# One denominator set per segment, gate rows behind the first logit slot, and numerators normalized on GpSimd in a gated mix of linear-memory attention and a GeGLU layer

## The chip, the cores and the metric

The kernel runs on one core of one Trainium2 chip. The metric is the device time of one execution in microseconds; the median of three runs of the kernel before is 274.99 us (274.38 to 275.15). PE is the matmul engine (TensorE), PEld its weight loads, DVE VectorE, ACT ScalarE, POOL GpSimd, and SP the engine that issues most of the transfers.

## The reference

`x` is 2048 x 512 in bfloat16. The output is `g * a + (1 - g) * b`, with a gate per row, an attention part `a` and a feed-forward part `b`:

```python
g = _sigmoid((x * gate_w).sum(-1, keepdims=True))
h = _gelu(x @ w_gate) * (x @ w_up)                 # 512 -> 1792
b = h @ w_down                                     # 1792 -> 512
# attention: 32 heads of 16, four segments of 512 rows, head gate sigmoid(beta)
for s in range(N):                                 # N = 4
    logits = jnp.einsum('bhqd,bhkd->bhqk', qs, ks) * scale + mask   # causal in the segment
    a_dot = jnp.einsum('bhqk,bhkd->bhqd', _softmax(logits, axis=-1), vs)
    pq = phi(qs)                                   # t + 1 where t > 0, else exp(t)
    num = jnp.einsum('bhld,bhde->bhle', pq, M)
    den = jnp.einsum('bhld,bhd->bhl', pq, z)[..., None] + 1e-06
    outs.append(gh * (num / den) + (1.0 - gh) * a_dot)
    M = M + jnp.einsum('bhld,bhle->bhde', phi(ks), vs)
    z = z + jnp.einsum('bhld->bhd', phi(ks))
a = concat(outs) @ wo
```

`M` (16 x 16 per head) and `z` (16 per head) carry the memory over the segments; segment 0 has no memory part.

## The kernel before

**A schedule made at build time.** The kernel adds tasks with `add(engine, cost, fn, prio, deps, alloc, frees)` and lets `Sched.plan` simulate the five engines with these costs; `emit` writes the tasks in the planned order. Each engine then runs its own instructions strictly in that order. What is written before the tasks (memsets, masks, first loads) stands ahead of all tasks in its engine's queue. `NUPS` says how many of the 56 up groups are filler work in each segment, `SEED` perturbs priorities, and `RINGS` gives the number of buffers of each ring tile. `ps` is the whole PSUM, eight banks that the planner hands out.

**Stage 1 (to about 66 us).** x of segment 0 is transposed on PE against an identity (L550); DVE and ACT copy the result into `xT` (L316, two copies each), and 16 matmuls (L565) compute the keys of segment 0. Then follow q, v, and the 28 pairs of gate projections with their GELU on ACT (L475, L647). Among them stand one small matmul for the head gates (L666: `hot8` spreads the eight rows of `beta8` onto 128 rows) and, ahead of the pairs of segment 3, the 16 matmuls of the row gates (L601: `gwB` is gate_w, repeated 32 times). DVE transposes the row gates (L610), POOL spreads them over the partitions with 32 small copies into `G2` and `omz` (L618, L619), and ACT applies the exponential at the start of stage 2 (L624, L625).

**Stage 2 (66 to 260 us).** 80 logit slots: four segments, four chunks of eight heads, five slots each. In a slot, four 32-row strips of the array compute logits of four heads (L735, mode "row"); ACT takes the exponential into `pT` (L757), and POOL zeroes what the causal mask excludes (L766). Between the slots PE does filler groups (L479) in which four matmuls, each for 32 output columns of the array, run side by side: up projections (`wup`), the down projection with `wo` behind it into the same bank, and q, k, v of the next segments. Every fifth slot opens two `pv` groups (L785), which need the masked `pT`; DVE transposes their result, divides by its sum, adds the memory part and transposes it into `xT`.

**The memory part.** `phi` makes pq and pk with an exponential on ACT and two DVE operations, `m_update` accumulates `M` and `z` in `Macc` and writes them, masked by block, into `Mbd` and `zbd`. `mem_den` is a dense product of the four chunks of pq with `zbd`, all accumulated into one bank: 4 chunks x 4 column strips = 16 matmuls. `mem_num` makes four matmuls per chunk with `Mbd`. The numerators are transposed on DVE into `Tm` (L977) and multiplied there with the reciprocal denominators `rm` (L981).

**Loads.** SP issues the weights in the order written, then gate_w, beta, `wup`, `wo` and, once the first transposes are done, `wdn`. `f_wo` scales `wo` by one minus the head gate on DVE (L681).

Of the kernel before, what the change touches and what calls it, by code (L numbers as in the profile page):

```python
# [10 lines left out]
ALU = mybir.AluOpType  # L11
# [26 lines left out]
NUPS = (28, 10, 9, 9)  # L38
ATT = 5
SEED = 1  # L40
# [248 lines left out]
def kernel(  # L289
# [22 lines left out]
    def copy(e, dst, src):  # L312
        if e == "ACT":
            nc.scalar.activation(dst, src, AF.Copy)
        else:
# [6 lines left out]
    RINGS = {"qT": 3, "kT": 3, "kO": 3, "pT": 12, "E": 1, "Q1": 1, "pq": 3,  # L322
             "pkT": 1, "pk": 2, "T": 2, "r": 2, "N": 2, "rm": 1, "Tm": 1, "Nm": 3,
             "osb": 3, "tt": 1}
# [34 lines left out]
    beta8 = ctile("beta8", [8, NCH])  # L359
    bd = ctile("bd", [P, 8, DH])  # L360
    hot8 = ctile("hot8", [8, 8, DH])
# [3 lines left out]
    zbd = ctile("zbd", [P, NCH * (P + 2)])  # L365
# [5 lines left out]
    omg = ctile("omg", [P, NCH], F32)  # L371
    ebr = ctile("ebr", [P, NCH], F32)
    tb = ctile("tb", [P, NCH], F32)
# [13 lines left out]
    gwB = p1.tile([P, FC, 32], BF, name="gwB", tag="gwB")  # L387
# [4 lines left out]
    nc.vector.memset(warm, 0.0)  # L392
    x0r = x2[0:L, :].rearrange("(kt p) d -> p kt d", p=P)
# [11 lines left out]
    nc.sync.dma_start(beta8[:, :], A_beta.rearrange("(c h) -> h c", h=8))  # L405
    load_w(nc.sync, wup, B_w_up)
    load_w(nc.sync, wo, A_wo)

    def ext(at):
# [17 lines left out]
    nc.vector.memset(zbd[:, :], 0.0)  # L427
# [8 lines left out]
                            compare_op=ALU.is_ge, fill=0.0, base=DH - 1, channel_multiplier=-1)  # L436
    nc.gpsimd.memset(vz[1][:, :, :], 1.0)
# [158 lines left out]
    def gate_rows(prio):  # L596

        def mms(t):
            for fc in range(FC):
                for s in range(NSEG):  # L600
                    nc.tensor.matmul(t[32 * s:32 * s + 32, :], lhsT=gwB[:, fc, :],  # L601
                                     rhs=xT[:, fc, s * L:(s + 1) * L], start=(fc == 0),
                                     stop=(fc == FC - 1), tile_position=(0, 32 * s),
                                     skip_group_check=True)
        g, box = group("gz", 4 * MM, mms, prio, a_x + [TAB["gwB"]], mode="col")
        tl = {}

        def f_tt(e, t):
            tl["tt"] = rtile("tt", [P, QB, 32], F32, p1)
            nc.vector.transpose(tl["tt"][:, :, :].rearrange("p a b -> p (a b)"), t[:, :])  # L610

        def f_sp(e):
            z = tl["tt"]
            for s in range(NSEG):
                src = slice(32 * s, 32 * s + 32)
                for j in range(4):
                    dst = slice(32 * j, 32 * j + 32)
                    nc.gpsimd.tensor_copy(G2[dst, s, :], z[src, :, 0])  # L618
                    nc.gpsimd.tensor_copy(  # L619
                        omz[dst, s, :],  # L620
                        z[src, :, :].rearrange("p (kt a) b -> p a kt b", a=4)[:, j, :, 0])

        def f_ex(e):
            nc.scalar.activation(G2[:, :, :], G2[:, :, :], AF.Exp)  # L624
            nc.scalar.activation(omz[:, :, :], omz[:, :, :], AF.Exp)  # L625

        def f_om(e):
            nc.vector.tensor_scalar_add(omz[:, :, :], omz[:, :, :], 1.0)
            nc.vector.reciprocal(omz[:, :, :], omz[:, :, :])
        for s in range(NSEG):  # L630
            read_x[s].append(g)
        tt = evac("DVE", g, box, f_tt, alloc=["tt"])
        TAB["zsp"] = add("POOL", 4000, f_sp, deps=[tt], prio=6, frees=[("tt", tt)])

        def later():
            TAB["g2"] = add("ACT", 500, f_ex, deps=[TAB["zsp"], TAB["first_x"]], prio=2)
            TAB["omz"] = add("DVE", 250, f_om, deps=[TAB["g2"]], prio=5)
        TAB["later"] = later
# [26 lines left out]
    def f_bps(t):  # L665
        nc.tensor.matmul(t[:, 0:NCH], lhsT=hot8[:, :, :].rearrange("p a b -> p (a b)"),  # L666
                         rhs=beta8[:, :], start=True, stop=True)
# [5 lines left out]
    def f_eb(e):  # L673
        nc.vector.reciprocal(ebr[:, :], omg[:, :])
        nc.vector.tensor_scalar_add(ebr[:, :], ebr[:, :], -1.0)
        for c in range(NCH):
            nc.vector.tensor_scalar_mul(bdeb[:, c, :, :], bd[:, :, :], ebr[:, c:c + 1])

    def f_wo(e):
        for c in range(NCH):  # L680
            nc.vector.tensor_scalar_mul(wo[:, c, :], wo[:, c, :], omg[:, c:c + 1])  # L681
# [6 lines left out]
    for s in range(NSEG):  # L688
        if s == 3:
            gate_rows(-960 + 20 * s)  # L690
        for hp in range(HS // 2):
            gate_pair(s, hp, -959 + 20 * s + hp)
            if s == 1 and hp == HS // 2 - 1:
                g, box = group("bps", 60, f_bps, -922, [a_be])
                t_tb = evac("ACT", g, box, lambda e, t: nc.scalar.activation(
                    tb[:, :], t[:, 0:NCH], AF.Tanh, scale=0.5), cost=250)
                t_om = add("DVE", 100, f_omg, deps=[t_tb], prio=5)
                t_eb = add("DVE", 1200, f_eb, deps=[t_om], prio=5)
                t_wo = add("DVE", 1300, f_wo, deps=[t_om, a_wo], prio=7)
# [4 lines left out]
    opened = add("EXT", 0, reopen, deps=list(GM.values()) + [TAB["zsp"]])  # L704
# [3 lines left out]

    def lhs_rhs(s, c, e, j, kt, qb, nq):
        pr, i = c // 2, c % 2  # L710
        a = slice(32 * j, 32 * j + (DH if e == 0 else 32))
        k = QK[("k" if e == 0 else "o", s, pr)]
        return (k[a, i, kt * P:(kt + 1) * P],
                QK[("q", s, pr)][a, i, qb * P:(qb + nq) * P])

    def logit_slot(s, t):
# [20 lines left out]
        deps = [EVQK[("q", s, c)]]  # L737
        if w <= 2:
            deps.append(EVQK[("k", s, c)])
        if w >= 2:  # L740
            deps.append(EVQK[("o", s, c)])
# [5 lines left out]
        if w == 4 and c % 2 == 1:  # L747
            pr = c // 2
            frees = [(n + "T" if n != "o" else "kO", first_ev[(n, s, pr)]) for n in "qko"]
            if s == 0:  # L750
                frees = [((r, pr) if r == "kT" else r, x) for r, x in frees]
# [22 lines left out]
    def pv_group(s, c, e):  # L774
# [4 lines left out]
        def mms(t):  # L779
            for w, kt, qb, nq, at in ((w0, 0, 0, 4, 0), (w0 + 1, 1, 1, 2, 0),  # L780
                                      (w0 + 1, 1, 3, 1, 3), (2, 2, 2, 2, 2 * e),
                                      (w0 + 1, 3, 3, 1, 2)):
                for j in range(4):
                    h = 8 * c + 2 * j + e
                    nc.tensor.matmul(t[32 * j:32 * j + 32, qb * P:(qb + nq) * P],  # L785
# [3 lines left out]
                                     tile_position=(0, 32 * j), skip_group_check=True)  # L789
# [52 lines left out]
    def phi(src, deps, prio, mk, ring):  # L842
# [7 lines left out]
        def f_q(_):  # L850
            box["Q"] = rtile("Q1", [P, 2, L])
            nc.vector.tensor_scalar(out=box["Q"][:, :, :], in0=src()[:, :, :], scalar1=0.0,
                                    scalar2=1.0, op0=ALU.max, op1=ALU.add)

        def f_a(_):
            nc.vector.tensor_tensor(mk()[:, :, :], box["E"][:, :, :], box["Q"][:, :, :],
                                    op=ALU.min)
        e = add("ACT", 960, f_e, prio=prio, deps=deps + [TAB["first_x"], opened], alloc=["E"])
        q = add("DVE", 325, f_q, port=True, prio=5, deps=[e], alloc=["Q1"])
        return add("DVE", 602, f_a, port=True, prio=5, deps=[q], alloc=[ring],  # L860
                   frees=[("E", e), ("Q1", q)])

    def phi_q(s, pr, prio):
# [3 lines left out]
        PHI[("q", s, pr)] = phi(lambda: QK[("q", s, pr)],  # L867
                                [EVQK[("q", s, 2 * pr)], EVQK[("q", s, 2 * pr + 1)]], prio, mk, "pq")

    def phi_k(s, pr, prio):  # L870
# [5 lines left out]
        p = phi(lambda: QK[("k", s, pr)],  # L876
# [7 lines left out]
        PKD[(s, pr)] = add("SP", 2400, f_d, deps=[p], alloc=["pk"], frees=[("pkT", p)], lat=2600)  # L884

    def m_update(s, pr, prio):
# [34 lines left out]
        def f_zbd(_):  # L921
            nc.vector.tensor_mul(
                zbd[:, :].rearrange("p (c n) -> p c n", c=NCH)[:, :, 0:P]
                .rearrange("p c (j m) -> p c j m", j=4)[:, :, :, 0:2],
                Macc[:, :, :, DH][:, :, None, :].to_broadcast((P, NCH, 4, 2)),
                bd[:, :, 0].rearrange("p (j e) -> p j e", j=4)[:, None, :, :]
                .to_broadcast((P, NCH, 4, 2)))
# [5 lines left out]
    def mem_den(s, prio):  # L933
        bx = {}

        def mms(t):
            for c in range(NCH):
                dense(t, zbd[:, c * P:(c + 1) * P], PQ[(s, c // 2)][:, c % 2, :], c == 0,
                      c == NCH - 1)
        g, box = group("den", 4 * MM, mms, prio,  # L940
                       [TAB[("zbd", s - 1)], PHI[("q", s, 0)], PHI[("q", s, 1)]],
                       also=("Tm", lambda: bx.update(Td=rtile("Tm", [P, QB, 32], F32))),
                       frees=[("pq", PHI[("q", s, pr)]) for pr in range(2)])
# [21 lines left out]
    def mem_num(s, c, prio):  # L965
        def mms(t):
            dense(t, Mbd[:, c, :, :].rearrange("p h d -> p (h d)"), PQ[(s, c // 2)][:, c % 2, :],
                  True, True)
        bx = {}
        g, box = group("num", MM, mms, prio,  # L970
                       TAB[("mbd", s - 1)] + [TAB[("den", s)], PHI[("q", s, c // 2)]],
                       also=("Tm", lambda: bx.update(T=rtile("Tm", [P, QB, 2, DH], F32))),
                       frees=[("pq", PHI[("q", s, c // 2)])])
# [5 lines left out]
        def f_n(_):  # L979
            NMt[(s, c)] = rtile("Nm", [P, QB, 2, DH])  # L980
            nc.vector.tensor_mul(NMt[(s, c)][:, :, :, :], bx["T"][:, :, :, :],  # L981
# [3 lines left out]
        NMT[("Nm", (s, c))] = add("DVE", 593, f_n, port=True, prio=2.5, deps=[ev, TAB[("rm", s)]],  # L985
# [44 lines left out]
    def fillers(s):  # L1030
# [10 lines left out]
        if s < NSEG - 1:  # L1041
            phi_k(s, 0, ph)
            for pr in range(2):
                for which in "kq":
                    for c in (2 * pr, 2 * pr + 1):
                        qk_group(s + 1, c, which, n1 + 5 * c - 8, AE)
# [12 lines left out]
    for s in range(NSEG):  # L1059
        for t in range(NSLOT):  # L1060
            logit_slot(s, t)
            if TAB["first_x"] is None:
                TAB["first_x"] = XT_[(0, 0)]
                TAB["later"]()
# [40 lines left out]
```

## Time and profile before

| | before |
|---|---|
| median of three runs | 274.99 us (274.38 to 275.15) |
| profiled execution, its own time | 274.56 us |
| its span, first to last instruction | 272.7 us |
| PE busy | 266.6 us, 98% |
| ACT, DVE, POOL busy | 211.6, 171.5, 106.2 us |
| granted TensorE clock | 1.00 |
| bytes moved | 14.02 MB, mean 51 GB/s |

The page lists busy time by engine, then the chain of work that ended last, followed back from the last instruction. The timeline lists instructions with start, duration, engine, line, operation, output and inputs, and in brackets the engine's idle time before and what ended it. Line numbers are those of the kernel before.

### The profile page before, as it was taken

The numbers are of one execution on the slowest core, as the hardware profiler recorded it, in microseconds if no ns is written. First come the engines' busy times: TensorE is split into PE (matmuls) and PEld (weight loads), VectorE is DVE, ScalarE is ACT, GpSimd is POOL, SyncE is SP. The second block draws the span as 40 slices with busy tenths as digits, with TensorE's granted clock in tenths as the row PEclk, the third lists the DMA queues.
The fourth block names the chain that finished last, engine by engine and source line by source line (L and its number), as shares of the span: only waits on it lengthen the run. The fifth ranks groups of instructions, "written<-read, shape, count | busy, mean of one in ns | idle before, by whom it ended". The sixth has DMA issues, their size and how long they took to land.

```text
span 272.7 us, 10273 instructions
## 1 busy us (share of the span) xinstructions
PE 266.6 (98%) x4569; PEld 127.0 (47%) x4575; DVE 171.5 (63%) x323; ACT 211.6 (78%) x234; POOL 106.2 (39%) x209
## 2 busy tenths in 40 slices
PE   7999999999999999999999999999999999999995
PEld 4444444444444554454444454444444444444454
DVE  3340003000888898989998989999858698765140
ACT  3445555646987799998978998899998999889812
POOL 8100000070343444355444545455555456664500
PEclk9999999999999999999999999999999999999999
DMA  7994790000023000220001121000000000000002
GB/s 210 369 135 97 256 352 10 0 0 2 5 45 38 2 2 2 41 43 2 2 23 22 42 41 41 5 2 2 22 22 4 22 24 2 22 22 22 22 5 78
DMA packets 22244, 14.02 MB, mean 51 GB/s; under 512 B 14136, under 2 KB 21176, under 8 KB 22200
## 3 DMA queue, kind: packets, MB, share of 16 engines
q1 hardware_dynamic: 21624, 12.85, 17.9%
q8 instruction: 35, 0.57, 0.9%
q10 hardware_dynamic: 576, 0.52, 0.6%
q14 instruction: 9, 0.07, 0.1%
HBM read 8.13 MB, written 2.10 MB: 37 GB/s over the span
## 4 chain that ended last, share of the span: by engine, by line
PE 97%; ACT 1%; issue 1%; DVE 0%; ACTq 0%
PE ps L479 57%; PE ps L475 20%; PE ps L735 10%; PE ps L785 6%; PE ps L565 1%; PE ps L529 1%; ACT pT L757 1%; PE ps L894 1%; PE ps L550 0%; PE ps L601 0%; DVE xT L316 0%; ACT osb L1017 0%; DVE wdn L392 0%; PE ps L666 0%; ACTq L1017 0%
## 5 line engine op out<-in xcount | busy, mean ns | idle before, releaser
L757 ACT ACTIVATE pT<-ps 128x1024 bf16<-128x1024 f32 x160 | 153.7, 1031 | 15.9 <-PE ps L735 14.7
L766 POOL TENSOR_SCALAR_AFFINE_SELECT pT<-pT 128x512 bf16<-128x512 bf16 (+1 forms) x160 | 94.3, 592 | 104.0 <-ACT pT L757 103.2
L479 PE MATMUL ps<-wdn,G 128*32 128x512 bf16 (+1 forms) x952 | 59.1, 368 | 0.2 <-ACT pT L757 0.2
L479 PE MATMUL ps<-xT,wup 128*32 128x512 bf16 x896 | 55.5, 380 | 0.0
L657 DVE TENSOR_TENSOR G<-ps,G 128x512 bf16<-128x512 f32 x56 | 37.8, 680 | 18.3 <-PE ps L479 18.0
L475 PE MATMUL ps<-xT,wga 128*128 128x512 bf16 x219 | 48.4, 379 | 0.4 <-issue 0.2
L647 ACT ACTIVATE G<-ps 128x1024 bf16<-128x1024 f32 x28 | 28.7, 1024 | 23.5 <-PE ps L475 22.8
L475 PEld LDWEIGHTS <-wga 128*128 128x128 bf16 x224 | 21.7, 98 | 26.4 <-issue 0.4
L803 DVE STREAM_TRANSPOSE T<-ps 128x512 f32<-128x512 f32 x32 | 22.7, 708 | 17.7 <-PE ps L785 11.6
L479 PEld LDWEIGHTS <-wup 128*32 128x32 bf16 x896 | 23.2, 96 | 21.1 <-issue 2.1
L479 PEld LDWEIGHTS <-G 128*32 128x32 bf16 x952 | 22.4, 96 | 19.4 <-issue 4.2
L618 POOL COPY G_87<-tt 32x16 f32<-32x16 f32 x16 | 3.1, 195 | 47.8 <-DVE tt L610 47.2
L735 PE MATMUL ps<-qT,kT 16*128 16x256 bf16 (+2 forms) x320 | 17.4, 274 | 0.0
L735 PE MATMUL ps<-qT,kO 32*128 32x128 bf16 (+2 forms) x320 | 17.3, 272 | 0.0
L479 PE MATMUL ps<-wo,xT 128*32 128x512 bf16 (+1 forms) x272 | 16.5, 367 | 0.0
L479 PEld LDWEIGHTS <-xT 128*32 128x32 bf16 x464 | 11.5, 96 | 10.3 <-issue 2.1
L735 PEld LDWEIGHTS <-kT 16*128 16x128 bf16 x320 | 6.8, 92 | 18.9 <-issue 18.8
L735 PEld LDWEIGHTS <-kO 32*128 32x128 bf16 x320 | 6.9, 92 | 12.1 <-issue 12.0
L479 PE MATMUL ps<-xT,wq 128*32 128x512 bf16 x192 | 12.5, 380 | 0.0
L479 PE MATMUL ps<-xT,wk 128*32 128x512 bf16 x192 | 12.5, 380 | 0.0
L1017 ACT ACTIVATE osb<-ps,omz 128x512 bf16<-128x512 f32 (+1 forms) x8 | 5.1, 635 | 9.4 <-PE ps L479 9.4
L479 PE MATMUL ps<-wv,xT 128*32 128x512 bf16 x192 | 12.4, 381 | 0.0
(116 smaller groups left out, 249.6 us busy)
## 6 DMA issues: line engine op xcount, KB each, us to landing
out_dram<-osb SPq DMA_DIRECT2D x15, 128.0 KB, 1.8
wup<-in_B_w_up_dram SPq DMA_DIRECT2D x1, 1792.0 KB, 8.2
wdn<-in_B_w_down_dram SPq DMA_DIRECT2D x1, 1792.0 KB, 13.7
wga<-in_B_w_gate_dram SPq DMA_DIRECT2D x1, 1280.0 KB, 10.2
wq<-in_A_wq_dram SPq DMA_DIRECT2D x1, 512.0 KB, 4.8
wga<-in_B_w_gate_dram SPq DMA_DIRECT2D x1, 512.0 KB
wv<-in_A_wv_dram SPq DMA_DIRECT2D x1, 512.0 KB, 7.3
wo<-in_A_wo_dram SPq DMA_DIRECT2D x1, 512.0 KB, 9.3
```

The source lines that it names most:

```text
L475: nc.tensor.matmul(t, lhsT=lhsT, rhs=rhs, start=start, stop=stop)
L479: nc.tensor.matmul(t[a, :], lhsT=lhsT[:, a], rhs=rhs, start=start, stop=stop, tile_position=(0, 32 * j), skip_group_check=True)
L529: nc.tensor.matmul(pair(w)[:, 0, :], lhsT=warm[:, 0:P], rhs=warm, start=True, stop=True)
L618: nc.gpsimd.tensor_copy(G2[dst, s, :], z[src, :, 0])
L647: ge = evac("ACT", g, box, lambda e, t: nc.scalar.activation(dst, t[:, :, :], AF.Gelu_apprx_tanh), cost=920, ring="pair")
L657: UPT[(s, hs)] = evac("DVE", g, box, lambda e, t: nc.vector.tensor_mul(G[:, s, hs, :], t[:, :], G[:, s, hs, :]))
L735: nc.tensor.matmul(A[j // 2][:, j % 2, at * P:(at + nq) * P], lhsT=l, rhs=r, start=True, stop=True, tile_position=(32 * j, 0))
L757: nc.scalar.activation(pT[(s, t, h)][:, :, :], A[h][:, :, :], AF.Exp, scale=0.25)
L766: nc.gpsimd.affine_select(out=v, in_=v, pattern=pat, compare_op=ALU.is_ge, fill=0.0, base=0, channel_multiplier=-1)
L785: nc.tensor.matmul(t[32 * j:32 * j + 32, qb * P:(qb + nq) * P], lhsT=vz[s % 2][:, kt, h * VW:h * VW + 32], rhs=pT[(s, t0 + w, j // 2)][:, ...
L803: nc.vector.transpose(TT[key][:, e, :, :].rearrange("p a b -> p (a b)"), t[:, :])
L1017: nc.scalar.activation(bx["o"][:, cols], bank(first)[:, cols], AF.Copy, scale=f)
```

## The change

1. *Denominators.* Slot c of a segment no longer takes the four head pairs of chunk c but one head pair from each chunk: strip j uses chunk (c + j) mod 4. A column strip q of `mem_den` and `mem_num` then needs chunk q of pq alone. `zbd` shrinks to 32 columns per chunk, and `mem_den` becomes four matmuls that run side by side into one bank. `mem_num` keeps four matmuls per set. A mask `zmask` for `zbd` is made by 16 DVE copies from `bd`, written ahead of all tasks.
2. *Rows of wo.* They follow the new order of heads: 16 loads of 32 rows in the place of one; the head gates are needed in both orders, so `beta8` gets 16 small loads more, is cleared by a memset, and has 128 rows, as has `hot8`.
3. *Gate rows.* They move from stage 1 behind the first logit slot; their spreading on POOL becomes four tasks, and `Tm` serves as their buffer.
4. *Numerators.* Their normalization moves from DVE to POOL.
5. *Rings and schedule.* `qT`, `kT`, `kO` have four buffers instead of three, `pq` two instead of three, `Q1` and `tt` go; `phi` works in place; the first slot of a segment waits for all q, k and odd-k of the segment; the q and k groups get earlier priorities; `NUPS` and `SEED` change.

```diff
-NUPS = (28, 10, 9, 9)
+NUPS = (27, 9, 9, 11)
-SEED = 1
+SEED = 3
...
+    nc.vector.memset(beta8[:, :, :], 0.0)
...
+    bsrc = A_beta.rearrange("(q j e) -> j e q", j=4, e=2)
+    nc.sync.dma_start(beta8[0:8, 0, :], A_beta.rearrange("(c h) -> h c", h=8))
+    for q in range(4):
+        for g in range(NCH):
+            nc.sync.dma_start(beta8[2 * q:2 * q + 2, 1, g:g + 1], bsrc[(q - g) % 4, :, q:q + 1])
     load_w(nc.sync, wup, B_w_up)
-    load_w(nc.sync, wo, A_wo)
+    for q in range(4):
+        for g in range(NCH):
+            r0 = P * q + 32 * ((q - g) % 4)
+            nc.sync.dma_start(wo[32 * q:32 * q + 32, g, :], A_wo[r0:r0 + 32, :])
...
+    for q in range(4):
+        for g in range(NCH):
+            j = (q - g) % 4
+            a = slice(32 * j, 32 * j + 32)
+            nc.vector.tensor_copy(zmask[a, q, 2 * g:2 * g + 2], bd[a, 2 * j:2 * j + 2, 0])
...
-        tt = evac("DVE", g, box, f_tt, alloc=["tt"])
-        TAB["zsp"] = add("POOL", 4000, f_sp, deps=[tt], prio=6, frees=[("tt", tt)])
+        tt = evac("DVE", g, box, f_tt, deps=[opened], alloc=["Tm"])
+        sp = [add("POOL", 1000, f_sp(s), deps=[tt], prio=6, frees=[("Tm", tt)])
+              for s in range(NSEG)]
+        TAB["g2"] = add("ACT", 500, f_ex, deps=sp + [TAB["first_x"]], prio=2)
+        TAB["omz"] = add("DVE", 250, f_om, deps=[TAB["g2"]], prio=5)
...
-        pr, i = c // 2, c % 2
+        pr, i = divmod((c + j) % 4, 2)
...
-            for c in range(NCH):
-                dense(t, zbd[:, c * P:(c + 1) * P], PQ[(s, c // 2)][:, c % 2, :], c == 0,
-                      c == NCH - 1)
+            for q in range(4):
+                nc.tensor.matmul(t[32 * q:32 * q + 32, :], lhsT=zbd[:, q, :],
+                                 rhs=PQ[(s, q // 2)][:, q % 2, :], start=True, stop=True,
+                                 tile_position=(0, 32 * q), skip_group_check=True)
...
-            nc.vector.tensor_mul(NMt[(s, c)][:, :, :, :], bx["T"][:, :, :, :],
+            nc.gpsimd.tensor_mul(NMt[(s, c)][:, :, :, :], bx["T"][:, :, :, :],
...
-        NMT[("Nm", (s, c))] = add("DVE", 593, f_n, port=True, prio=2.5, deps=[ev, TAB[("rm", s)]],
+        NMT[("Nm", (s, c))] = add("POOL", 1150, f_n, prio=2.5, deps=[ev, TAB[("rm", s)]],
...
-                        qk_group(s + 1, c, which, n1 + 5 * c - 8, AE)
+                        qk_group(s + 1, c, which, n1 - 10 + 1.5 * c, AE)
...
-                TAB["later"]()
+                gate_rows(-5)
```

## The prediction

> **What bounds the kernel now.** I read the engine rows of the page first, then the chain of work that ended last, then the first ten microseconds of the timeline, and last the stretches of the timeline in which the change puts something. The engine rows of the page (busy us, share, instructions) and its chain by engine:
>
> ```profile
> PE 266.6 (98%) x4569; PEld 127.0 (47%) x4575; DVE 171.5 (63%) x323; ACT 211.6 (78%) x234; POOL 106.2 (39%) x209
> ...
> PE 97%; ACT 1%; issue 1%; DVE 0%; ACTq 0%
> ```
>
> PE is 97% of the chain. A busy PE need not be at its peak, so I look whether the chain's pieces are at a steady price (start, duration, what):
>
> ```profile
> 5.30 0.70 DVE xT L316
> 6.05 3.61 PE ps L565 x16
> ...
> 53.04 0.98 PE ps L601 x16
> 54.17 10.74 PE ps L475 x49
> ...
> 73.59 2.70 PE ps L479 x48
> ...
> 83.09 0.86 PE ps L479 x16
> ```
>
> A set of four 32-column matmuls of 512 costs 0.86/4 = 0.215 us; 48 of them after a logit slot cost 2.70 = 12 x 0.215 + 0.12, so the change of array layout after a slot costs about 0.12. With these prices the 2648 wide and 144 half-width matmuls of L479 give 662 x 0.215 + 36 x 0.108 + 80 x 0.12 = 156 us (one change back for each of the 80 slots), and the chain gives L479 56.9% of 272.7 = 155 us. No hidden stretch is left inside PE's work: a set removed is worth 0.215 us, relief of another engine is worth nothing by itself, and every microsecond for which PE waits after 6.05 us comes out at the end. Only 0.74 us of PE is idle between 66 and 260 us.
>
> Where PE starts its real work (start, duration, engine, line, what):
>
> ```profile
> 4.47 1.53 DVE L316 CAST xT<-ps 128x512 bf16<-128x512 f32 x2 [2.05 <-PE ps L550]
> ...
> 5.02 0.34 POOL L435 TENSOR_SCALAR_AFFINE_SELECT bd<-bd 128x128 bf16<-128x128 bf16 x1
> ...
> 6.05 3.61 PE L565 MATMUL ps<-xT,wk 128*128 128x512 bf16 x16 [0.56 <-DVE xT L316]
> ```
>
> DVE's two casts of xT release the first projection. POOL finishes bd only at 5.36 us, because the memset of vz (1.89 to 3.85 us) stands before it in its queue. Prices for what is added and moved, from the timeline (DVE at 29 and 184 us, POOL at 55 to 61 us):
>
> ```profile
> 29.05 0.44 DVE L662 COPY gwB<-gw 128x32 bf16<-128x32 bf16 x4 [11.75 <-DMA gw<-in_gate_w_dram]
> ...
> 54.95 0.19 POOL L618 COPY G_87<-tt 32x16 f32<-32x16 f32 x1 [47.22 <-DVE tt L610]
> ...
> 60.58 0.18 POOL L619 COPY omz<-tt 32x4 f32<-32x4 f32 x1
> ...
> 184.62 0.88 DVE L918 TENSOR_TENSOR Mbd<-Macc,bdeb 32x128 bf16<-32x128 f32 x3
> ```
>
> **The change, part by part.** The sum is made against this execution's 274.56 us (span 272.7), 0.43 below the median of the runs, 274.99.
>
> Denominators. Per segment 1 to 3, 16 matmuls become 4: nine sets, 9 x 0.215 = 1.94 us less on PE. The numerators keep four matmuls per set.
>
> Gate rows. Before, they change the array layout twice amid full-size work: 53.04 to 54.17 us is 1.13 for 0.86 of work. Behind the first logit slot the change back is paid anyway: 0.27 less. So PE loses 2.21 us of work.
>
> The masks at the start. DVE gets 16 copies (32x2, into zmask) ahead of its xT casts, and the first waits for bd on POOL, 5.36 us instead of no wait at all. Queued behind them on DVE are the casts, and behind the casts PE's L565. The copy itself is not in the trace. Successive ones start on different partition groups; L918 does that too, and there three take 0.88 with a median of 0.284 each, so each starts when the one before has ended. Tiny DVE rows last 0.16 to 0.18 (L628 165 ns, gwB 178 ns): 16 x 0.165 = 2.64. If they overlapped as gwB's do (0.087 apart), 1.5; if neighbours on POOL stretched them to 0.22, 3.5. Casts back to back took 1.29 at 9.27 us (kT). 5.41 + 2.64 + 1.29 + 0.05 = 9.39 instead of 6.05: I take +3.3, ends +2.2 and +4.2. PE is then idle from 5.48 to 9.39 us. The transposed x and wk are there by 6.0, so nothing hides it.
>
> PE's speed after that gap. The granted clock is 1.00 throughout, yet the six L529 matmuls, from 1.26 us on, are 0.43 us apart and the 16 of L565 0.226 (3.61/16): PE begins slow, and was slow for about 3.9 us (1.26 to some 5.2, where the matmuls of L550 shorten from 314 to 219 ns). A gap of 0.56 us kept it fast; one of 3.9 is nearer to the idle before the start. Ends: 0, and another slow stretch of 3.9 us at half speed, +1.95. I take the middle, +1.0. The Trainium skill (TensorE: Matmul & The Clock Gate, section on the HAM clock gate) says that one idle window of about 3.4 us halves the array clock and one busy window restores it; by that rule the estimate for this term would be about +1.7, and the sum 0.7 higher.
>
> The wait behind the gate rows. Counted from the first logit slot (66.14 before): PE ends the gate rows at 1.3; DVE's transposition and POOL's start follow 0.93 later, as at 54.02 to 54.95. POOL's 32 spreading copies took 5.81 us for 32, 0.183 each. In the new order 16 stand ahead of the first two masks of pT (L766, 0.41 each) and 16 behind: 2.24 + 2.93 + 0.82 + 2.93 = 8.9. ACT's exponential of G2 now sits behind pT of the second slot, done at 7.4, and holds ACT until 9.3; pT of the third slot is queued behind it. PE's fourth slot takes banks 0 and 1, which that pT frees: not at 9.1 but at 10.3. On DVE omz waits for the same exponential, and behind it stand pkT and two products G, one of which frees the bank of the next k group: 9.25 + 0.42 + 0.69 + 0.69 = 11.1 instead of 9.4. I take +1.7. Before, these copies cost nothing, since gate matmuls covered them (54 to 66 us). Ends: 0, if the bank is free anyway; +2.5, if pv's masks come later still.
>
> Normalization on POOL. 12 products leave DVE (L981, 855 ns, 10.3 us together), worth nothing by PE's chain. On POOL the product is not in the trace: nearest are the selects of 128x512 (L766, mean 714 ns), below, and two of them, 1.4, above, as it reads two float inputs. POOL is busy 94 of 194 us in the attention stretch (66 to 260 us); 12 x 1.05 (the middle) and 5.8 of copies make it 113. But pv's masks are queued behind each product, and each product waits for DVE's Tm. Ends: -0.7 (PE's idle 0.51 and 0.23 us at 224 and 234 us go, since the last segment gets two more up groups as filler) and +2 (three pv groups each late by a whole select). I take 0. The Trainium skill (GPSIMD Engine Reference, section 3.1) speaks against this move: it gives two-input elementwise work there about 2.6 cycles of 1.2 GHz per element and calls VectorE the place for it. An estimate from that is 1.1 us a piece; by it the sum stays as it is.
>
> DMAs. SP gets 16 small beta loads before wup and 16 loads for wo instead of one. SP's issues took 0.37 to 0.58 (26.16 to 28.41 us): beta ends near 26.8 + 17 x 0.45 = 34.4, landed by 37.5; the product of beta stood at 40.67 and will stand 4 us later. wup is issued 7 us later, landed near 43, used from 70; wo near 50, scaled on DVE while it idles until 66; wdn 14 us later, used after 110. At nothing; if the loads cost 1 us each, PE would wait 1 to 2 us for beta. The beta product is one matmul as before (173 ns). The other rings, the mapping of heads onto rows and the new order of groups change no count: 80 slots, the same projections; the q and k groups now run a segment ahead of their slots. At nothing, cover being PE's fixed order; the last term's ends hold it.
>
> Sum: 274.56 - 2.21 + 3.3 + 1.0 + 1.7 + 0 = 278.3 (278.35 before rounding).
>
> **The rivals.** (1) The start alone counts: PE stays fast and the gate rows' wait is half covered: 274.56 - 2.21 + 3.3 + 0.85 = 276.5. For it: nothing in the trace shows at which gap PE becomes slow, and the bank may be free by then; against it: the order in which ACT and DVE take their work. (2) POOL becomes the pacing queue: products of 1.4 us or more ahead of pv's masks hold PE in each segment, +2 more: 280.4. For it: ACT's masks feed pv directly in 160 places; against: POOL is only half busy. (3) The other side: small copies are cheaper in their new places than these rows say. Then the 16 on DVE cost about 0.062 each (end 6.4, casts 7.7, PE +1.7, the gap 2.3 us), and POOL's 32 stay under the 4 us that the new tasks reserve, so ACT does not wait and PE's 0.51 us at 224 us goes too: 274.56 - 2.21 + 1.7 - 0.51 = 273.5. It decides from about 0.09 us per copy on DVE and 0.12 on POOL downward; L918 and L618 speak against it, gwB's spacing for it. (4) The change does little: 2.2 of saved work meets only the start at its lower end, 274.6.
>
> **How the numbers follow.** Forecast 0.52 (278.3, own range 276.9 to 280.0), rival 1 0.20, rival 2 0.13, rival 3 0.08, rival 4 0.07. About 0.3% (0.8 us) can be told from no change. Faster 0.07 (rival 3), same 0.09 (rival 4 and the edge of 1), slower 0.84. The range leaves out most of rivals 3 and 4 and the far end of 2: 275.3 to 280.9.
>
> **What would show it.** zmask copies on DVE from 5.4 us, 0.16 apart, and L565's counterpart near 9.4 us; its matmuls 0.43 apart at first; POOL's spreading until some 9 us after the first slot, with ACT idle before G2's exponential and PE idle for 1 to 2 us around the fourth slot; 12 matmuls on zbd; POOL products between 0.7 and 1.4 us without PE waits behind them. I am wrong if L565 starts below 8 us, or if PE shows no idle time at the fourth slot.

## The result, and the profile after

The changed kernel takes 281.36 us (median of 4 runs, 281.22 to 281.8) against 274.94 of the kernel before: a ratio of 1.0239, 95% interval 1.022 to 1.0259. It is slower by 6.4 us, where 3.3 had been forecast; 281.36 lies 0.46 us above the range. The profiled execution took 281.46 us, 6.90 more than the one of before, with a span of 279.8 us.

The engine rows and the chain by engine, as on the page of the changed kernel:

```profile
PE 265.7 (95%) x4534; PEld 126.2 (45%) x4539; DVE 169.7 (61%) x328; ACT 212.1 (76%) x235; POOL 116.4 (42%) x221
...
PE 85%; DVE 6%; POOL 4%; ACT 3%; issue 1%; POOLq 0%; ACTq 0%; DVEq 0%
```

PE fell from 97% of the chain to 85%; DVE and POOL have entered it. Where they stand is in the timeline of the start (start, duration, engine, line, what):

```profile
5.04 0.34 POOL L446 TENSOR_SCALAR_AFFINE_SELECT bd<-bd 128x128 bf16<-128x128 bf16 x1
5.33 1.96 POOL L453 MEMSET vz_83<- 128x2240 bf16 x1
5.42 4.68 DVE L452 COPY zmask<-bd 32x2 bf16<-32x2 bf16 x16 [3.17 <-POOL bd L446]
7.23 0.52 POOL L454 MEMSET Mbd<- 128x512 bf16 x1
10.02 1.27 DVE L316 CAST xT<-ps 128x512 bf16<-128x512 f32 x2
...
11.34 5.20 PE L581 MATMUL ps<-xT,wk 128*128 128x512 bf16 x16 [6.22 <-DVE xT L316]
```

The 16 mask copies take 4.68 us, and L581, which was L565, starts at 11.34 instead of 6.05. Half of the 4.68 us is the first copy; the chain lists it by itself, beside the second one:

```profile
5.42 2.35 DVE zmask L452
...
7.78 0.17 DVE zmask L452
```

L581 also runs slower: 5.20 us instead of 3.61. The table of stretches (length, then PE's busy time; the last three numbers are the granted TensorE clock, the DMA share and GB/s) shows why:

```profile
7.75:14.58 6.83, 3.24 (x8) 1.13 (x8) 3.37 (x18) 0.00 (x0) 0.00 (x0) 0.50 1.17 352
...
5.00:11.30 6.30, 0.12 (x3) 0.10 (x1) 5.71 (x18) 0.80 (x2) 2.71 (x3) 0.72 0.98 315
11.30:14.70 3.40, 3.36 (x9) 1.18 (x9) 0.00 (x0) 0.00 (x0) 0.00 (x0) 0.52 1.33 348
14.70:16.60 1.90, 1.90 (x11) 0.84 (x10) 0.45 (x1) 0.67 (x2) 0.00 (x0) 1.00 1.06 197
```

While PE waited, at 7.75 us, the granted clock fell to half; it stayed there until 14.58, for 3.24 us of PE's work, and came back to 1.00. The other place is behind the first logit slot:

```profile
72.08 1.05 PE L617 MATMUL ps<-xT,gwB 128*32 128x512 bf16 x16
...
73.96 0.19 POOL L634 COPY G_89<-Tm 32x16 f32<-32x16 f32 x1 [66.21 <-DVE Tm L626]
...
80.75 0.19 POOL L635 COPY omz<-Tm 32x4 f32<-32x4 f32 x1
80.83 0.26 ACT L641 ACTIVATE G_89<-G_89 128x64 f32<-128x64 f32 x1 [1.93 <-POOL G_89 L634]
...
81.87 0.90 DVE L867 TENSOR_TENSOR pkT<-E,pkT 128x1024 bf16<-128x1024 bf16 x1
82.16 0.40 PE L750 MATMUL ps<-qT,kO 32*128 32x512 bf16 x4 [1.09 <-ACT pT L767]
...
82.69 1.27 DVE L672 TENSOR_TENSOR G<-ps,G 128x512 bf16<-128x512 f32 x2
...
83.42 1.05 PE L495 MATMUL ps<-xT,wk 128*32 128x512 bf16 x16 [0.86 <-DVE G L672]
```

POOL needs until 80.9 us for its 32 copies, ACT idles 1.93 us for them, and PE waits 1.09 us at the fourth slot and 0.86 at the k group behind it.

By stage, from the two profiles:

| stretch | before, us | after, us | difference |
|---|---|---|---|
| to the start of the first projection | 6.05 | 11.34 | +5.29 |
| its 16 matmuls | 3.61 | 5.20 | +1.59 |
| from there to the first logit slot | 56.55 | 55.28 | -1.27 (the gate rows have left) |
| first logit slot to the end of the span | 206.5 | 208.0 | +1.5 |

In the last row stand 1.94 us less of denominators, 1.01 more of gate rows, and PE's idle time of 2.99 us (1.09, 0.86, 0.54, 0.50) against 0.74: together +1.3.

### The profile page after: what moved, and what is told of

Same layout as the page of the kernel before. It is cut to its first block, busy times and chain, and to the rows that moved or that the text cites. A ratio compares the mean times of both kernels' runs of the same rounds, so it can differ in the third digit from the quotient of the medians.

```text
span 279.8 us, 10233 instructions
## 1 busy us (share of the span) xinstructions
PE 265.7 (95%) x4534; PEld 126.2 (45%) x4539; DVE 169.7 (61%) x328; ACT 212.1 (76%) x235; POOL 116.4 (42%) x221
## 4 chain that ended last, share of the span: by engine, by line
PE 85%; DVE 6%; POOL 4%; ACT 3%; issue 1%; POOLq 0%; ACTq 0%; DVEq 0%
PE ps L495 48%; PE ps L491 20%; PE ps L750 8%; PE ps L796 6%; ACT pT L767 2%; PE ps L581 2%; DVE zmask L452 2%; POOL G_89 L634 1%; PE ps L975 1%; POOL omz L635 1%; POOL vz_82 L439 1%; PE ps L903 1%; DVE T L814 1%; DVE G L672 0%; DVE Tm L987 0%
## 5 line engine op out<-in xcount | busy, mean ns | idle before, releaser
L776 POOL TENSOR_SCALAR_AFFINE_SELECT pT<-pT 128x512 bf16<-128x512 bf16 (+1 forms) x160 | 91.6, 577 | 80.7 <-ACT pT L767 79.9
L495 PE MATMUL ps<-wdn,G 128*32 128x512 bf16 (+1 forms) x952 | 59.8, 368 | 0.0
L634 POOL COPY G_89<-Tm 32x16 f32<-32x16 f32 x16 | 3.4, 214 | 66.8 <-DVE Tm L626 66.2
L626 DVE STREAM_TRANSPOSE Tm<-ps 128x512 f32<-128x512 f32 x1 | 0.7, 716 | 22.0 <-PE ps L617 22.0
L991 POOL TENSOR_TENSOR Nm<-Tm,rm 128x512 bf16<-128x512 f32 x12 | 13.3, 1109 | 1.1 <-DVE N L837 0.9
```

Of the source, the lines that this page charges most:

```text
L495: nc.tensor.matmul(t[a, :], lhsT=lhsT[:, a], rhs=rhs, start=start, stop=stop, tile_position=(0, 32 * j), skip_group_check=True)
L776: nc.gpsimd.affine_select(out=v, in_=v, pattern=pat, compare_op=ALU.is_ge, fill=0.0, base=0, channel_multiplier=-1)
L991: nc.gpsimd.tensor_mul(NMt[(s, c)][:, :, :, :], bx["T"][:, :, :, :], RMt[s][:, :, 2 * c:2 * c + 2][:, :, :, None] .to_broadcast((P, QB, 2, ...
```

## The experiments

All ratios are to the kernel before, timed beside the run, with 95% intervals. No experiment leaves out a part of the computation; where matmuls are added, their results are overwritten. In all of them PE's order is that of the changed kernel, apart from matmuls that are added.

**1. POOL's memsets after the masks, first try.** The theory to be tested was that the first mask copy waits for an SBUF port that POOL's memsets hold; the rival, that the first copy is long for a reason of its own.

```diff
-    nc.gpsimd.memset(vz[1][:, :, :], 1.0)
-    nc.gpsimd.memset(Mbd[:, :, :, :], 0.0)
+    def f_ms(e):                       # the same two memsets
...
+    add("POOL", 2500, f_ms, deps=[a_gw], prio=3)
```

> The changed kernel, with POOL's memsets of the second vz buffer and of Mbd taken from the start to POOL's idle time after 27 us; the 16 mask copies stay where they are on DVE. Theory (the first copy's 2.35 us is a wait for an SBUF port that POOL's memsets hold until 7.75 us): the first copy takes 0.16 us like the others, the masks end near 7.9 us, L581 starts near 9.2 instead of 11.34, and the time falls by 2.1 us to 279.2, or to 277.7 if PE stays fast over the shorter gap. Rival (the first copy is long for a reason of its own, the wait for bd or the first of its form): 281.4, L581 at 11.3.

Measured: 281.54 us (281.43 to 283.91), ratio 1.0249 (1.0203 to 1.0294), and the memsets at 5.32 and 7.22 us as before: the planned time of a task makes nothing wait on the chip, and POOL had nothing ahead of them. The run says nothing on the question; its repetition is number 4.

**2. The masks sorted by partition group.**

```diff
-    for q in range(4):
-        for g in range(NCH):
-            j = (q - g) % 4
+    for j in range(4):
+        for q in range(4):
+            g = (q - j) % 4
```

> The changed kernel, with the same 16 mask copies in the same place, but sorted by partition group, so that the start partition changes 3 times instead of 15. Theory (a copy that starts on another partition group waits for the one before to end, 0.15 us; within a group they overlap to about 0.09): 12 x 0.06 = 0.7 us less, 280.6, and the first copy still 2.35 us. Rival (spacing is the copy's own price): 281.4, spacing 0.15 throughout.

Measured: 280.56 us, ratio 1.0217 (1.0162 to 1.0271). The time alone cannot tell 0.8 us; the trace can:

```profile
5.41 3.54 DVE L452 COPY zmask<-bd 32x2 bf16<-32x2 bf16 x16 [3.18 <-POOL bd L446]
...
10.33 5.27 PE L581 MATMUL ps<-xT,wk 128*128 128x512 bf16 x16 [4.62 <-DVE xT L316]
```

The longest copy is still 2.35 us. The first four copies, all on one partition group, follow each other 0.07 to 0.08 us apart and end together at 7.8 us; the twelve behind them need 1.16 us. Where the next copy starts on another group, the spacing is 0.17 us. The first order changed the group in 12 of 15 steps (the expectation counted 15), with 0.17 to 0.18 us at a change and 0.08 without. So the change of the partition group about doubles the spacing of tiny copies, and L581 starts 1.0 us earlier when there are fewer changes.

**3. PE kept busy in its wait.**

```diff
                                              rhs=ident, start=True, stop=True)
+                    if h == 1 and i == 1:
+                        for _ in range(26):
+                            nc.tensor.matmul(tl["k", 1][:, 1, :], lhsT=warm[:, 0:P], rhs=warm,
+                                             start=True, stop=True)
```

> The changed kernel, with 26 matmuls of zeros (128x512, into a bank that is overwritten later) put behind the transposes of x on PE, which fill its wait for the masks. Theory (PE's matmuls run slow after a gap of 6.2 us because it was idle): the 16 of L581 take 3.6 us instead of 5.2, the granted clock of the first stretch is 1.00 from 5 us on, 281.4 - 1.6 = 279.8. Rival (they are slow because their operands come late or are being written): L581 5.2 us as before, 281.4.

Measured: 280.12 us, ratio 1.0174 (1.0147 to 1.02).

```profile
5.50 6.39 PE L571 MATMUL ps<-wdn 128*128 128x512 bf16 x26
11.73 3.62 PE L585 MATMUL ps<-xT,wk 128*128 128x512 bf16 x16
```

The 16 matmuls take 3.62 us, as before the change: idleness had slowed them. The gain is 1.2 and not 1.6 us, since the added matmuls end 0.4 us after the casts.

**4. POOL really idle while the masks are made.**

```diff
-    nc.gpsimd.memset(vz[1][:, :, :], 1.0)
-    nc.gpsimd.memset(Mbd[:, :, :, :], 0.0)
+    def f_ms(e):
+        nc.vector.memset(vz[1][:, :, :], 1.0)
+        nc.vector.memset(Mbd[:, :, :, :], 0.0)
+    add("DVE", 2500, f_ms, deps=[a_gw], prio=4)
```

> The changed kernel, with POOL's memsets of the second vz buffer and of Mbd done by DVE, behind its copies of gwB in stage 1 (after 29 us), so that POOL is really idle while the 16 mask copies run in their place. In the run before this one they stayed where they were in time, since nothing in POOL's queue made them wait. Theory (the first copy's 2.35 us is a wait for an SBUF port that POOL's memsets hold): the first copy takes about 0.16 us, the masks end near 7.9 us, L581's counterpart starts near 9.2, the time falls by 2.1 us to about 279.2, by 3.7 if PE stays fast over the shorter gap. Rival (the first copy is long for a reason of its own): first copy 2.35 us, no change.

Measured: 281.44 us (279.04 to 282.21), ratio 1.0225 (1.0186 to 1.0263). The time did not move, the trace did:

```profile
5.42 2.49 DVE L452 COPY zmask<-bd 32x2 bf16<-32x2 bf16 x16 [3.18 <-POOL bd L446]
...
7.83 1.27 DVE L316 CAST xT<-ps 128x512 bf16<-128x512 f32 x2
...
9.15 6.44 PE L579 MATMUL ps<-xT,wk 128*128 128x512 bf16 x16 [3.88 <-DVE xT L316]
```

No copy is longer than 0.17 us now, and the projection starts at 9.15 us: the 2.2 us were a wait for POOL's memsets. That the two engines share a port is not shown by it. Why the time did not follow is in the stretches of the same execution:

```profile
8.09:14.92 6.83, 5.77 (x14) 2.08 (x14) 1.01 (x2) 0.03 (x1) 0.00 (x0) 0.50 1.15 321
...
79.77:83.18 3.41, 1.45 (x28) 0.69 (x24) 2.71 (x5) 3.29 (x6) 3.07 (x6) 1.00 0.03 7
83.18:86.60 3.42, 3.42 (x48) 1.81 (x44) 1.69 (x4) 1.67 (x2) 0.81 (x2) 0.50 0.68 80
```

The clock was half for 6.83 us, as long as in the changed kernel's profile, but PE was already at work for 5.77 us of them instead of 3.24, and 14 of the 16 matmuls ran slow instead of 8. So 0.9 of the 2.19 us are left when the projection is done (the next group starts at 15.43 against 16.38 us). Then the clock fell a second time, right behind the wait for the gate rows, where PE had been busy for only 1.45 of 3.41 us. The lead turned into a lag of 0.7 us (the slot behind it starts at 87.41 against 86.67), and this execution, the slowest of the four, took 282.21 us, 0.75 more than the changed kernel's profiled one. The profile of run 1 (283.91 us) has the same second fall, from 84.41 to 87.82 us; the changed kernel's has none, with the same waits. What decides it was not tested, and of the other three executions here no trace was kept.

**5. Both: POOL idle, PE busy.** The edit is that of 4 and that of 3, with 15 matmuls.

> The changed kernel with POOL's two memsets done by DVE later, so that the 16 mask copies need 2.5 us instead of 4.7, and with 15 matmuls of zeros on PE in the gap, so that it does not cool down. Theory (the port wait costs 2.2 us, which the run without the memsets showed at the start of L581 but gave back through slower matmuls behind it): L581's counterpart starts at 9.2 us and takes 3.6, the time is 281.4 - 2.2 - 1.6 = 277.6, and 2.2 us less than the run with PE kept busy alone (280.1 there). Rival (the port wait is no loss in time): 280.

Measured: 277.7 us, ratio 1.0118 (1.0095 to 1.014); the projection starts at 9.12 us and takes 3.6. With the clock held, the wait for the memsets shows its price: 2.4 us below run 3 by the medians. In the two profiles the projection starts 2.61 us earlier (9.12 against 11.73), of which 0.4 is the delay by run 3's own added matmuls and 2.2 the wait.

**6. The masks out of the way.**

```diff
+    def f_zm(e):                       # the 16 copies, unchanged
...
+    add("DVE", 2600, f_zm, deps=[a_gw], prio=4)
```

> The changed kernel, with the 16 mask copies moved from ahead of all tasks to DVE's idle time after 27 us; the order of PE, ACT and POOL and the rest of DVE is unchanged. Theory (the start costs 5.3 us of wait and 1.6 us of slow matmuls, all from these copies): L581 at 6.05 us in 3.6 us, 281.4 - 6.9 = 274.5, within 0.3% of the kernel before. Rival (part of the late start comes from the beta memset, from the wider hot8, or from the loads): L581 later than 6.3 us, 275.5 or more.

Measured: 275.84 us (274.5 to 277.16, 10 runs), ratio 1.0018 (0.9989 to 1.0048).

```profile
5.96 3.63 PE L576 MATMUL ps<-xT,wk 128*128 128x512 bf16 x16 [0.87 <-DMA wk<-in_A_wk_dram]
```

The start is that of the kernel before, now released by wk. The profiled execution took 274.5 us, 6.96 less than that of the changed kernel; the medians differ by 5.5, in runs that spread more than usual, as did those of the kernel before (274.58 to 277.17). So the whole loss of the start came from these copies; the remaining waits cancel the saved work. The spread has a pattern: five of the ten executions had a mean granted clock of 0.999 or 1.000 and a median of 274.76 us, the other five a clock of 0.994 and a median of 276.57. A stretch of 3.4 us at half clock, as in run 4, would make a mean of 0.994 and cost some 1.7 us (an estimate: half of 3.4). The profiled execution is one of the first five, so where the clock fell in the others is not shown.

**7. Fewer spreading copies.** On top of 6, POOL spreads only `G2`, and `omz` is made from it.

```diff
-                    nc.gpsimd.tensor_copy(omz[dst, s, :], ...)
-            nc.scalar.activation(omz[:, :, :], omz[:, :, :], AF.Exp)
-            nc.vector.tensor_scalar_add(omz[:, :, :], omz[:, :, :], 1.0)
+            for j in range(4):
+                a = slice(32 * j, 32 * j + 32)
+                nc.vector.tensor_scalar_add(
+                    omz[a, :, :],
+                    G2[a, :, :].rearrange("p s (kt a) -> p s kt a", a=4)[:, :, :, j], 1.0)
```

> The changed kernel with the 16 mask copies moved to DVE's idle time, and with POOL spreading only G2 (16 copies instead of 32): omz is then made by DVE from G2 behind the one exponential (four small additions); the order of PE is unchanged. Theory (ACT, and behind it PE, waits at the third and fourth slot for POOL's 32 copies, 1.95 us): POOL's copies are done some 2.9 us earlier, ACT does not wait before G2's exponential, PE's idle time around the fourth slot falls from 1.95 to under 0.3 us; 1.7 us below the kernel with the masks moved alone, about 273.5, 0.5% below the kernel before. Rival (PE's wait there comes from the logits' banks and ACT's own load, not from the copies): no change against the masks moved alone.

Measured: 273.93 us, ratio 0.997 (0.9957 to 0.9983). That is 1.9 us below run 6 by the medians, but only 0.8 below its five executions at full clock, as much as PE's idle time fell here (from 1.95 to 1.11 us).

```profile
72.24 0.26 ACT L633 ACTIVATE G<-G 128x64 f32<-128x64 f32 x1
...
73.05 1.40 DVE L638 TENSOR_SCALAR omz<-G 32x16 f32<-32x16 f32 x4
...
75.93 1.05 PE L490 MATMUL ps<-xT,wk 128*32 128x512 bf16 x16 [1.11 <-DVE G L667]
```

ACT no longer waits for POOL, and PE no longer waits at the fourth slot. At the k group it still does, 1.11 us, because the four additions are long themselves (1.40 us) and stand ahead of the product G whose bank is wanted. The expected 0.3 us of idle time was missed.

**8. The normalization back on DVE.** On top of 7.

```diff
-            nc.gpsimd.tensor_mul(NMt[(s, c)][:, :, :, :], bx["T"][:, :, :, :],
+            nc.vector.tensor_mul(NMt[(s, c)][:, :, :, :], bx["T"][:, :, :, :],
```

> As the kernel with both repairs (masks moved, 16 spreading copies), with the 12 normalizations of the numerators on DVE again, issued at the same place in the order of the program; PE's order unchanged. Theory (PE sets the time, DVE's relief is worth nothing by itself): within 0.7 us of the kernel with both repairs. Rival A (DVE's relief is what lets the new order run): slower by 2 us or more, with PE waiting for DVE's transpositions and products G. Rival B (POOL's products hold the masks of pT and through them pv): faster by 0.5 us or more.

Measured: 275.63 us, ratio 1.0029 (1.0015 to 1.0043): 1.7 us slower than 7, near rival A. In this kernel's timeline PE has three waits for DVE that 7 has not:

```profile
191.86 0.73 PE L799 MATMUL ps<-pT,vz 128*32 128x512 bf16 x20 [0.35 <-DVE vz L316]
...
220.15 0.29 PE L753 MATMUL ps<-qT,kT 16*128 16x256 bf16 x4 [0.45 <-DVE G L667]
...
224.81 0.73 PE L799 MATMUL ps<-pT,vz 128*32 128x512 bf16 x20 [0.25 <-DVE Tm L990]
```

At each of the three places it falls back by a further 0.5 us against 7. The order of the tasks was planned for a DVE without these products, so this prices the move within this order, not in general.

**9. The denominators four times.** On top of 7.

```diff
+            for _ in range(4):
                 for q in range(4):
                     nc.tensor.matmul(t[32 * q:32 * q + 32, :], lhsT=zbd[:, q, :],
```

> As the kernel with both repairs, with the four denominator matmuls of each segment issued four times over (the same values written again), 36 matmuls more in all: the PE work of the denominators as it was before the change. Theory (nine sets of four at 0.215 us lie on PE's path): 1.9 us slower than the kernel with both repairs. Rival (another engine sets the pace in those slots): less than 0.8 us slower.

Measured: 276.17 us, ratio 1.0061 (1.0039 to 1.0083), 2.2 us slower than 7; the profiled spans differ by 1.6 (273.9 against 272.3). Both lie around the 1.94 that was worked out.

**10. omz later.** On top of 7, the additions and the reciprocal stand behind DVE's last transposition of segment 0.

```diff
+            if key == (0, 3):          # in f_o, behind the transposition
+                for j in range(4):     # the four additions of 7
...
+                nc.vector.reciprocal(omz[:, :, :], omz[:, :, :])
```

> As the kernel with both repairs, with DVE's making of omz (four additions and a reciprocal, 1.65 us at the third slot) moved behind DVE's last transposition of segment 0; omz is first read in segment 1. PE's order unchanged. Theory (PE's remaining 1.11 us at the first k group is DVE's queue: omz and pkT stand ahead of the product G whose bank that group takes): PE's idle time there falls under 0.2 us, 1.0 us below the kernel with both repairs, 272.9, ratio to before 0.993. Rival (PE waits there for ACT's exponentials of the third slot through another bank): the idle time stays, no change.

Measured: 273.66 us, ratio 0.996 (0.9942 to 0.9977), 0.3 and not 1.0 us below 7. The wait of 1.11 us is gone, but there is a new one:

```profile
137.87 1.05 PE L490 MATMUL ps<-wv,xT 128*32 128x512 bf16 x16 [0.73 <-DVE vz L316]
```

**11. omz's additions on POOL.** As 10, with the four additions behind POOL's masks of the sixth slot.

```diff
+                if gi == 5 and h == 1:   # in fa, behind the mask
+                    for j in range(4):   # the four additions, nc.gpsimd
...
```

> As the run before it, with the four additions for omz on POOL, behind its masks of the sixth slot, where POOL is idle for 1 us or more between masks; only the reciprocal (0.25 us) stays on DVE behind the last transposition of segment 0. Theory (moving the additions on DVE only moved PE's wait, from the first k group to a v group of segment 1 at 137.9 us, 0.73): that idle time falls under 0.2 us and no new one appears, 0.6 us less, about 273.0. Rival (the wait at the v group is part of the new order and has nothing to do with omz): unchanged, 273.7.

Measured: 272.89 us, ratio 0.9931 (0.9917 to 0.9944). Between the first logit slot and the end only the waits of 0.54 and 0.50 us are left of more than 0.3. With its two new waits mended, the change is 1.9 us faster than the kernel before, and 8.5 faster than as it was made.

## Why the prediction was right and wrong

*The sets.* Right: the changed kernel's profile has 12 matmuls on `zbd` instead of 48, and 36 put back cost 2.2 us by the medians and 1.6 by the spans, against 1.94.

*Gate rows as PE work.* Forecast 0.27 less; they cost 1.13 in stage 1 and 1.01 now. Small, and not tested by itself.

*The masks at the start.* The step that failed. Place and chain were right (bd, copies, casts, first projection), and so was the spacing, 0.155 us on average against 0.165 (the prediction took all 15 steps to change the partition group; three do not). But the cost was taken as a sum of 16 durations, with an upper end of +4.2; measured is +5.29. What was missing is a wait of 2.2 us of the first copy behind POOL's two memsets, the first of which starts 0.09 us before it. The prediction had allowed for a stretching of every copy, not for one copy held until POOL is done. With that wait taken away (run 4) the start is +3.10, close to the +3.3 of the sum. The Trainium skill (GPSIMD Engine Reference, section 1, Specifications) says that GpSimd's SBUF interface is shared with VectorE and that DVE instructions in a two-port mode or with two SBUF inputs contend for it. Run 4 agrees: without the memsets the longest copy falls from 2.35 us to 0.17. In which mode the copy ran, no run shows. The DVE memsets at the start, which ran beside POOL's memset of the first vz in 0.07 and 0.11 us (0.28 for the larger one in the kernel before), show that not every DVE instruction waits.

*PE's speed after the gap.* Right in kind, forecast +1.0 of 0 to 1.95, measured +1.59; run 3 shows that idleness was the cause. The Trainium skill (TensorE: Matmul & The Clock Gate, section on the HAM clock gate) says that an idle window of about 3.4 us halves the clock and a busy one restores it; the prediction's estimate from that was 1.7. The trace agrees in kind: in a wait of 6.2 us the granted clock fell to half and stayed there for 3.24 us of work. But with a wait of 3.9 us it stayed there for 5.77 us of work (run 4), so 3.4 us of work did not always restore it.

*The wait behind the gate rows.* Right: +1.7 forecast, 1.95 measured, in the two places named, with ACT idle before the exponential and DVE's omz ahead of the product. Runs 7 and 11 confirm it. What the prediction did not think of is that PE can become slow here too: 3.4 us at half clock followed this wait in the profiles of runs 1 and 4. In none of the 47 executions of runs 7 to 11, where the wait is shorter or gone, is the mean clock under 0.998.

*POOL's products.* 1109 ns each, within 0.7 to 1.4, and no PE wait is put down to them. The term of 0 fits the profile: PE's other idle time went from 0.74 to 1.04 us. But "relief of another engine is worth nothing by itself" was too strong. In this order the products on DVE cost 1.7 us (run 8); the move is part of what lets the new order run.

*The loads.* Right: from 16.6 to 71.8 us PE is idle for 0.26 us in all.

The two forecasts outside 0 that were too small, the start by 2.0 and the clock by 0.6, add to 2.6 of the 3.1 us that were missing. The rest is made of terms of 0.3 us and less. Rivals 1, 3 and 4 fell: the start was longer than the 3.3, 1.7 and 2.2 us that they put on it. Rival 2 had a time near the measured one for a wrong reason.

## What to carry to other kernels

Instructions written ahead of a planned schedule are on the critical path of the start, and nothing in the planner sees them; look at the first microseconds of each engine's queue before anything else. When a small operation is put behind another engine's result, ask what that engine does at the same moment and whether one can hold up the other, not only how long the operation lasts. And a moved stage needs an engine that idles in its new place: 32 small copies that were free beside the gate matmuls cost PE 2 us a few microseconds later.

## What the runs showed of the hardware that was not expected

A DVE copy of 32 x 2 elements waited 2.2 us for two POOL memsets, the second of which (7.23 to 7.75 us) had started while the copy was waiting. Tiny DVE copies follow each other 0.17 to 0.18 us apart when the next one starts on another partition group, and 0.07 to 0.08 apart on the same one. A wait of PE need not be one long one to cost clock: behind two waits of 1.09 and 0.87 us, close together, the granted clock was half for 3.4 us in the profiles of runs 1 and 4, and stayed at 1.00 in the changed kernel's. And removing 2.2 us of wait ahead of PE's first work left only 0.9 us when the projection was done, because the clock was half for 6.83 us either way and PE only met more of it, 14 slow matmuls instead of 8; with PE kept busy the removal was worth the whole 2.2 us.
